# Keys, queries and values stored in DRAM in their SBUF layout, one transfer a tile

## The chip, the cores and the metric

The kernel runs on one core of a Trainium2 chip. The metric is device time in microseconds of one execution, the median over several runs. One further execution was recorded by the hardware profiler; all rows in this document come from such recordings. Arranging the inputs in DRAM is done on the host before the launch and is not in the time.

## The reference

An attention layer with a bias made by a small network, followed by two feed-forward layers. Cut to what matters here:

```python
# q, k, v: (batch 2, heads 8, seq 576, head_dim 64), float32
scores = np.matmul(q, k.transpose(0, 1, 3, 2)) / sqrt(D)
x = (psi_rel / psi_i)[..., None]            # 576 x 576, from positions alone
h = np.maximum(x @ w1 + b1, 0.0)            # hidden 32
bias = h @ w2                               # 576 x 576 x 8 heads
attn = softmax(scores + bias.transpose(2, 0, 1)[None])
x = np.matmul(attn, v)                      # -> (1152 tokens, 512)
x = (silu(x @ w_gate) * (x @ w_val)) @ w_out      # d_ff 1536
out = softplus(x @ w_in) @ w_out2                 # d_ff 2048
```

## The kernel before

The kernel has three stages. **The bias stage** (up to about 64 us) makes the 8 x 576 x 576 bias in 36 steps. A step takes four hidden tiles `r` of 128 x 576: three made by VectorE (L260), one by ScalarE (L258), each from the table `G`; 12 such tiles exist, so the hidden tiles run at most three steps ahead. TensorE multiplies them with the second layer's weights into a PSUM tile `pb` (L268, two buffers). ScalarE then copies `pb`, scaled, into a staging tile (L280, "the keep"), and a DMA on the SyncE queue spreads the 128 staged rows over the bias tiles (L284; the first four steps, which go to the bias of the mixed chunk, take two DMAs each, L287). There are six staging tiles, the halves of `early4` to `early6`, used in turn: a keep waits until the DMA of the keep six steps earlier has landed. The steps 23, 26, 31 and 33 (counted from 0) also carry one of the attention's chunks each.

**The attention stage** (to about 196 us) works through 8 units, each a pair of heads of one batch, in 72 chunks: scores (L304 for the first two units, L331 for the others), bias and row maximum (L352), exponential (L366), normalizing (L374), transposes (L401), values (L428). **The feed-forward stage** (196 us to the end) is a chain of matmuls with weights that the SyncE queue brings in (L628). The order on each engine in the bias and attention stages is the order in which the code is written.

A unit needs three kinds of input. `load` (L161 to L165) brings keys or queries of both heads into a tile of 128 partitions x 2 heads x 576: partitions 0 to 63 and 64 to 127 get the same 64 rows, by two DMAs of 64 partitions (`load_k` into `kr` or, from the third unit on, into a part of the first bias tile, so rows named `bias<-in_kT_dram` are key loads; `load_q` into `qr` or `early7`, which shows as `early<-in_qT_dram`). `load_v` (L181 to L184) brings 512 rows of the values into `v` and the last 64 into `vt`. All go through the one SyncE queue, in the order of the code: the table `G`, then keys, queries and values of the first unit, keys and queries of the second, then the 40 bias DMAs of the 36 steps, then the loads of the later units, each a chunk or more ahead of its use. The completion counters of the DMAs are used in turn, eight of them, so a DMA is issued only when the one eight issues earlier has landed (`DMAHW0` to `DMAHW7` in the rows of the order below).

Of the kernel before, what the change touches and what calls it, by code (L numbers as in the profile page):

```python
# [19 lines left out]
P = 128  # L20
B, H, S, D, HID = 2, 8, 576, 64, 32
NP = H // 2
# [27 lines left out]
ROWS = np.r_[:256, 512:S, 256:512]  # L50
# [47 lines left out]


@with_exitstack  # L100
def tile_kernel(ctx: ExitStack, tc, qT, kT, vS, wb, wg, wv, wo, wi, wo2, table, out):
    nc = tc.nc
    sp = nc.sync
    const = ctx.enter_context(tc.tile_pool(name="const", bufs=1))
# [24 lines left out]
    with ExitStack() as actx:  # L129
# [29 lines left out]
        psS = pool("psS", 2, space=PSUM)  # L159

        def load(r, src, pr, b):  # L161
            for d in range(2):
                sp.dma_start(
                    out=r[D * d : D * (d + 1)], in_=src[b, 2 * pr : 2 * pr + 2].rearrange("h d s -> d h s")
                )  # L165

        def load_k(i):
            pr, b = UNITS[i]
            kr = kp.tile([P, 2, S], F32, tag="kst", name="kr") if i < PLAIN else bias[0][:, :2]
            load(kr, kT, pr, b)  # L170
            return dict(i=i, pr=pr, b=b, kr=kr)

        def load_q(u):
            u["qr"] = early[3] if u["i"] == 1 else qraw.tile([P, 2, S], F32, tag="qr", name="qr")
            load(u["qr"], qT, u["pr"], u["b"])

        def load_v(u):
            pr, b = u["pr"], u["b"]
            v = u["v"] = vp.tile([P, 4, 3 * D], F32, name="v")
            vt = u["vt"] = vts[u["i"] % 3]  # L180
            sp.dma_start(out=v, in_=vS[b, pr, :512].rearrange("(c p) e -> p c e", p=P))  # L181
            thirds = lambda ap: ap.rearrange("p (t e) -> p t e", t=3)
            sp.dma_start(out=thirds(vt[:D])[:, ::2], in_=thirds(vS[b, pr, 512:])[:, ::2])
            sp.dma_start(out=vt[D:, D : 2 * D], in_=vS[b, pr, 512:, D : 2 * D])  # L184

        def high(h, src, by="a"):
            if by == "a":
# [298 lines left out]
        units, late = [load_k(0)], []  # L486
        load_q(units[0])
        load_v(units[0])
        units.append(load_k(1))
        load_q(units[1])  # L490
# [7 lines left out]
        def run_slot():  # L498
            nonlocal turned, done, prep, before, slot
            if slot < len(chunks):  # L500
                i, sub, n = chunks[slot]
                if n == 0:
                    for _ in prep:
                        pass
                    if (i, sub) == (1, 0):
                        load_v(units[1])
                    elif (i, sub) == (0, 1):
                        units.append(load_k(2))
                    elif sub and i + 1 < 2 * NP:
                        load_q(units[i + 1])  # L510
                        if i > 1:
                            load_v(units[i + 1])
                        prep = itertools.chain(prepare_k(units[i + 1]), prepare_q(units[i + 1], 0))
                    elif i > 1 and not sub:
                        if i + 1 < 2 * NP:
                            units.append(load_k(i + 1))
                        if i == 2:
                            load_v(units[2])
                            units[2][0].update(v=units[2]["v"], vt=units[2]["vt"])
                        prep = prepare_q(units[i], 1)  # L520
                    if i < PLAIN:
                        job(units[i], sub)
                    if i == NP and sub == 0:
                        flat = lambda ap: ap.rearrange("p a s -> p (a s)")
                        pairs[2:] = [flat(bias[c][:, 2 * a : 2 * a + 2]) for a in range(2) for c in (2, 3)]
                        mixes[1] = flat(bias[4][:, :2])[:, : 5 * P]
                        nc.gpsimd.memset(mixes[1][:, S:], 0.0)
                u = units[i][sub]
                got = scores(u, n)
# [106 lines left out]
    def as_float(n):  # L636


        x = cvp.tile([P, 2 * NK, P], F32, tag="x", name="x")
        load(2 * n + 3)  # L640
        for j in range(2):
            raw, y = loaded[2 * n + j], x[:, NK * j : NK * (j + 1)]
            hw, lw, yi = raw[:, :, :, 1], raw[:, :, :, 0], y.bitcast(I32)
            if n < NL2:
                nc.scalar.activation(y, hw.bitcast(F32), AF.Prelu, scale=2.0**-112, alpha=-(2.0**32))
            else:
                nc.scalar.activation(y, hw.bitcast(F32), AF.Copy, scale=2.0**-112)  # L647
            nc.vector.tensor_scalar(yi, yi, 3, None, op0=ALU.logical_shift_left)  # L648
            if n >= NL2:
                nc.vector.scalar_tensor_tensor(yi, hw, -(2**31), yi, op0=ALU.bitwise_and, op1=ALU.bitwise_or)  # L650
            nc.vector.scalar_tensor_tensor(yi, lw, 29, yi, op0=ALU.logical_shift_right, op1=ALU.bitwise_or)  # L651
            load(2 * n + j + 4)
        return x
# [340 lines left out]
    for k in range(2):  # L994
        t4 = row()
        h, l = [ap.bitcast(F32) for ap in X["T2"][k]]
# [50 lines left out]
    with tc.manual_schedule(engines={E.PE}):  # L1047
        quads = {"z": z}
        for q in range(4):
# [5 lines left out]
            for word in f"{OTHER if q else FIRST} {TAIL}".split():  # L1055
                who, what = word
                if who in "tu":
# [7 lines left out]
                    for i, t in enumerate(TOKENS[n]):  # L1065
                        if who == "t":
                            continue
                        a, ps = acc[t // 2][:, t % 2], held[n][:, i]
# [12 lines left out]
                getattr(quads[who], "p" + what)()  # L1081


_INS = ["qT", "kT", "vS", "wb", "wg", "wv", "wo", "wi", "wo2", "table"]


# [32 lines left out]
```

## Time and profile before

| | us |
|---|---|
| median of 3 runs | 596.39 (596.32 to 596.82) |
| the profiled execution | 596.96 |
| its span, first to last instruction | 595.0 |
| bias stage: last keep starts at | 63.07 |
| attention stage: about | 64 to 196 |
| feed-forward stage: about | 196 to 592 |

The profiled execution is 0.57 us above the median, and 1.96 us of it lie outside the span. Over the whole span TensorE is recorded as busy 97% of the time, VectorE 76%, ScalarE 63%, GpSimd 17%. These are averages over three stages with different limits, so the slices of the span and the tables by stretch say more than the averages.

### The profile page before, as it was taken

Reading aid. Unit: us, or ns where it says so; the run is one execution under the profiler, and the core shown is the slowest. Engines: PE = TensorE matmul, PEld = TensorE weight load, DVE = VectorE, ACT = ScalarE, POOL = GpSimd, SP = SyncE. Lnnn points to the kernel's source line nnn. Section 1 sums busy time; section 2 is a strip of 40 time slices with the busy share of each in tenths; the row PEclk is TensorE's granted clock in tenths of the full one; section 3 lists DMA queues with packets and bytes.
Section 4 is the critical chain, followed back from the end, with each engine's and each line's share of the span. In section 5 each row is a group of like instructions: output and inputs, shape, how many; then the busy total and the mean of one; then the engine's idle time right before and its main releaser. Section 6 shows DMA issues by size and latency. Waiting matters only on the chain.

```text
span 595.0 us, 11346 instructions
## 1 busy us (share of the span) xinstructions
PE 578.5 (97%) x4274; PEld 506.3 (85%) x4274; DVE 454.2 (76%) x972; ACT 375.5 (63%) x711; POOL 98.8 (17%) x147
## 2 busy tenths in 40 slices
PE   8789999999999999999999999999999999999997
PEld 5233569888887999999999999999989989988986
DVE  6799687788888999897789735679998976983432
ACT  6699877778988876665558424349735734733520
POOL 0000477778993000000000000000000000000000
PEclk9899999999999999999999999999999999999999
DMA  9999924334442333324226222222444240310012
GB/s 216 223 204 210 192 80 108 97 88 111 110 128 82 121 96 110 101 79 135 72 89 194 72 72 72 74 83 64 135 138 136 81 142 8 136 35 1 2 54 105
DMA packets 47414, 63.30 MB, mean 106 GB/s; under 512 B 4480, under 2 KB 35200, under 8 KB 47360
## 3 DMA queue, kind: packets, MB, share of 16 engines
q1 hardware_dynamic: 47216, 62.57, 38.2%
q8 instruction: 33, 0.54, 0.4%
q14 instruction: 21, 0.17, 0.1%
q10 hardware_dynamic: 144, 0.02, 0.0%
HBM read 49.60 MB, written 2.36 MB: 87 GB/s over the span
## 4 chain that ended last, share of the span: by engine, by line
PE 83%; DMA 6%; DVE 5%; ACT 3%; issue 1%; POOL 1%; SPq 0%; ACTq 0%; DVEq 0%; POOLq 0%
PE pw L726 37%; PE pw L1034 17%; PE pw L677 13%; PE po L428 6%; PE ps L331 4%; DMA bias<-early 4%; PE pt L401 3%; DMA early<-in_qT_dram 1%; PE pb L268 1%; PE ps L304 1%; DMA qr<-in_qT_dram 1%; ACT early L280 1%; DVE e L352 1%; ACT e L366 1%; DVE bias L352 0%
## 5 line engine op out<-in xcount | busy, mean ns | idle before, releaser
L1034 PE MATMUL pw<-oh,g2h 128*128 128x512 f32 x144 | 56.2, 390 | 0.0
L1034 PE MATMUL pw<-oh,g2l 128*128 128x512 f32 x144 | 56.2, 390 | 0.0
L1034 PE MATMUL pw<-ol,g2h 128*128 128x512 f32 x144 | 56.1, 390 | 0.0
L268 PE MATMUL pb<-r,wb_sb 128*32 128x288 f32 x576 | 46.6, 426 | 7.8 <-ACT early L280 6.8
L260 DVE TENSOR_SCALAR r<-G 128x576 f32<-128x576 f32 x108 | 47.7, 516 | 4.3 <-PE pb L268 4.0
L268 PEld LDWEIGHTS pb<-r,wb_sb 128*32 128x32 f32 x576 | 18.8, 112 | 34.6 <-ACT early L280 18.9
L677 PE MATMUL pw<-gl,sh 128*128 128x384 f32 x144 | 48.2, 335 | 0.0
L677 PE MATMUL pw<-gh,sl 128*128 128x384 f32 x144 | 48.2, 334 | 0.0
L677 PE MATMUL pw<-gh,sh 128*128 128x384 f32 x144 | 48.2, 334 | 0.0
L651 DVE SCALAR_TENSOR_TENSOR x<-raw,x 128x512 int32<-128x512 int32 x68 | 46.3, 688 | 0.9
L374 POOL TENSOR_SCALAR e<-e,sm 128x576 f32<-128x576 f32 x44 | 34.4, 793 | 73.2 <-DVE sm L371 66.9
L352 DVE CUSTOM_DVE_ANT_0 e<-ps,bias 128x576 f32<-128x576 f32 x44 | 33.0, 750 | 13.2 <-PE ps L331 7.6
L408 ACT COPY at<-pt 128x512 f32<-128x512 f32 (+2 forms) x69 | 36.4, 547 | 6.4 <-PE pt L401 5.9
L331 PE MATMUL ps<-kst,ql 128*128 128x288 f32 x120 | 37.0, 337 | 2.0 <-DVE sm L352 1.4
L428 PE MATMUL po<-at,v 128*64 128x256 f32 (+3 forms) x384 | 36.8, 332 | 1.0 <-DVE at L408 0.8
L1072 DVE TENSOR_TENSOR acc<-pw,acc 128x512 f32<-128x512 f32 x27 | 17.5, 686 | 25.1 <-PE pw L1034 25.1
L366 ACT ACTIVATE e<-e,sm 128x576 f32<-128x576 f32 x44 | 34.3, 780 | 2.7 <-DVE sm L352 1.7
L648 DVE TENSOR_SCALAR x<-x 128x512 int32<-128x512 int32 x68 | 28.8, 428 | 9.3 <-ACT x L647 5.1
L428 PEld LDWEIGHTS po<-at,v 128*64 128x64 f32 x384 | 26.7, 137 | 8.2 <-issue 1.3
L331 PE MATMUL ps<-kst,qh 128*128 128x288 f32 x120 | 32.1, 295 | 0.0
L1034 PEld LDWEIGHTS pw<-oh,g2l 128*128 128x128 f32 x144 | 27.0, 188 | 5.8
L401 PE MATMUL pt<-ident,e 128*128 128x128 f32 x188 | 31.6, 276 | 0.1
(269 smaller groups left out, 1657.4 us busy)
## 6 DMA issues: line engine op xcount, KB each, us to landing
raw<-in_wo_dram SPq DMA_DIRECT2D x28, 512.0 KB, 3.5
bias<-early SPq DMA_DIRECT2D x32, 288.0 KB, 7.5
raw<-in_wi_dram SPq DMA_DIRECT2D x16, 512.0 KB, 3.8
raw<-in_wv_dram SPq DMA_DIRECT2D x12, 512.0 KB, 4.5
raw<-in_wg_dram SPq DMA_DIRECT2D x12, 512.0 KB, 3.5
qr<-in_qT_dram SPq DMA_DIRECT2D x14, 288.0 KB, 4.1
bias<-in_kT_dram SPq DMA_DIRECT2D x12, 288.0 KB, 4.6
v<-in_vS_dram SPq DMA_DIRECT2D x8, 384.0 KB, 3.6
```

What stands on the lines that cost most here:

```text
L260: nc.vector.tensor_scalar(r, G[:, w0 : w0 + S], PB[:, n : n + 1], 0.0, op0=ALU.add, op1=ALU.max)
L268: nc.tensor.matmul(pb[32 * ct : 32 * ct + 32, hf, :HALF], W2, rs[ct][:, HALF * hf : HALF * (hf + 1)], start=True, stop=True,)
L331: nc.tensor.matmul(ps[:, hf, :HALF], u[t][:, o : o + P], kst[:, a, HALF * hf : HALF * (hf + 1)], start=i == 0, stop=i == len(parts) - 1,)
L352: nc.vector.tensor_tensor_reduce(out=e[:, :S].rearrange("p (a n) -> p a n", a=2), in0=ps[:, :, :HALF], in1=bt.rearrange("p (a n) -> p a n" ...
L366: nc.scalar.activation(e, e, AF.Exp, bias=sm[:, 0, n : n + 1], scale=-1.0, accum_out=sm[:, 1, n : n + 1])
L401: nc.tensor.transpose(pt[:, P * w : P * (w + 1)], e, ident)
L408: marks[eng, u["i"], u["sub"]] = copy(at[:, :w], pt[:, :w]).ins
L428: nc.tensor.matmul(u["po"][D * a : D * (a + 1), o : o + n], v[:, D * t : D * (t + 1)], at[:, i : i + n], start=piece == 0 and o == 0, stop ...
L651: nc.vector.scalar_tensor_tensor(yi, lw, 29, yi, op0=ALU.logical_shift_right, op1=ALU.bitwise_or)
L677: nc.tensor.matmul(ps[:, :n], w[:, k], x, start=first and k == 0 and i == 0, stop=last and k == NK - 1 and i == 2)
L726: nc.tensor.matmul(ps[:, hf, :HALF], a[:, o + k], b[:, HALF * hf : HALF * (hf + 1)], start=start and k == 0 and i == 0, stop=k == 1 and i ...
L1034: nc.tensor.matmul(ps, g, w.rearrange("p k f -> p (k f)"), start=f == 0 and i == 0, stop=f == 3 and i == 2)
```

## The change

The host stores keys and queries for each batch and head pair as 128 rows of 1152 numbers (64 rows, written twice), values as 128 rows of 768 numbers, and the last 64 value rows as a tensor of their own, `vT`. A load of keys or queries becomes one DMA of 128 partitions with one run of 4608 bytes a partition, where there were two DMAs of 64 partitions with two runs of 2304 bytes each. The DMA into `v` keeps its 128 partitions, and its runs go from four of 768 bytes to one of 3072. The two DMAs into `vt` keep their shape. Keys and queries take twice the room in DRAM; as many bytes as before are read.

```diff
         def load(r, src, pr, b):
-            for d in range(2):
-                sp.dma_start(
-                    out=r[D * d : D * (d + 1)], in_=src[b, 2 * pr : 2 * pr + 2].rearrange("h d s -> d h s")
-                )
+            sp.dma_start(out=r, in_=src[b, pr].rearrange("p (h s) -> p h s", h=2))
...
-            sp.dma_start(out=v, in_=vS[b, pr, :512].rearrange("(c p) e -> p c e", p=P))
+            sp.dma_start(out=v, in_=vS[b, pr].rearrange("p (c e) -> p c e", c=4))
             thirds = lambda ap: ap.rearrange("p (t e) -> p t e", t=3)
-            sp.dma_start(out=thirds(vt[:D])[:, ::2], in_=thirds(vS[b, pr, 512:])[:, ::2])
-            sp.dma_start(out=vt[D:, D : 2 * D], in_=vS[b, pr, 512:, D : 2 * D])
+            sp.dma_start(out=thirds(vt[:D])[:, ::2], in_=thirds(vT[b, pr])[:, ::2])
+            sp.dma_start(out=vt[D:, D : 2 * D], in_=vT[b, pr, :, D : 2 * D])
...
+    vs = np.concatenate([v[:, ::2], np.roll(v[:, 1::2], -D, 2), v[:, 1::2]], 3)
+
+    def twice(a):
+
+        a = a.reshape(B, NP, 2, S, D).transpose(0, 1, 4, 2, 3).reshape(B, NP, D, 2 * S)
+        return np.concatenate([a, a], 2)
+
...
-        "qT": np.stack([q[:, h][:, ROWS if h % 2 else slice(None)] for h in range(H)], 1).transpose(0, 1, 3, 2),
-        "kT": k.transpose(0, 1, 3, 2),
-        "vS": np.concatenate([v[:, ::2], np.roll(v[:, 1::2], -D, 2), v[:, 1::2]], 3),
+        "qT": twice(np.stack([q[:, h][:, ROWS if h % 2 else slice(None)] for h in range(H)], 1)),
+        "kT": twice(k),
+        "vS": vs[:, :, :512].reshape(B, NP, 4, P, 3 * D).transpose(0, 1, 3, 2, 4).reshape(B, NP, P, 12 * D),
+        "vT": vs[:, :, 512:],
```

On TensorE, VectorE, ScalarE and GpSimd the same instructions stand in the same order; only the DMA counters that they wait on differ. The SyncE queue has 14 rows fewer. Its start before the change, from the first key load to the second bias DMA of the first step (`kr` keys, `qr` and `early` queries, `bias<-early` the bias of the steps; the rows with x2 are the two halves):

```order
L163 DMA kr<-in_kT_dram 64x2x576 x2
L163 DMA qr<-in_qT_dram 64x2x576 x2
L181 DMA v<-in_vS_dram 128x4x192
L183 DMA vt_96<-in_vS_dram 64x2x64 [waits DMAHW0_49,Pool_49]
L184 DMA vt_96<-in_vS_dram 64x64 [waits DMAHW1_49]
L163 DMA kr<-in_kT_dram 64x2x576 [waits DMAHW2_49]
L163 DMA kr<-in_kT_dram 64x2x576 [waits DMAHW3_49]
L163 DMA early_116<-in_qT_dram 64x2x576 [waits DMAHW4_49]
L163 DMA early_116<-in_qT_dram 64x2x576 [waits DMAHW5_49]
L287 DMA bias_89<-early_113 16x4x576 [waits DMAHW6_49,Activation_49]
L287 DMA bias_89<-early_113 16x4x576 [waits DMAHW7_49]
```

And the same place after it:

```order
L162 DMA kr<-in_kT_dram 128x1152
L162 DMA qr<-in_qT_dram 128x1152
L178 DMA v<-in_vS_dram 128x768
L180 DMA vt_96<-in_vT_dram 64x2x64 [waits Pool_49]
L181 DMA vt_96<-in_vT_dram 64x64
L162 DMA kr<-in_kT_dram 128x1152 [waits DMAHW0_49]
L162 DMA early_116<-in_qT_dram 128x1152 [waits DMAHW1_49]
L284 DMA bias_89<-early_113 16x4x576 [waits DMAHW2_49,Activation_49]
L284 DMA bias_89<-early_113 16x4x576 [waits DMAHW3_49]
```

Four issues went away, and each load stands behind an older DMA in the turn of the counters: the second unit's queries (`early`) waited for a landing of the first unit's queries and now wait for the first part of the table `G`.

## Rows read from the trace of the kernel before

**Rows 1.** The page, chain that ended last: shares of the span by engine.
```profile
PE 83%; DMA 6%; DVE 5%; ACT 3%; issue 1%; POOL 1%; SPq 0%; ACTq 0%; DVEq 0%; POOLq 0%
```
**Rows 2.** The page: 40 slices of 14.9 us, TensorE clock and DMA share in tenths.
```profile
PEclk9899999999999999999999999999999999999999
DMA  9999924334442333324226222222444240310012
```
**Rows 3.** Windows: each engine's busy us (instructions), granted clock, DMA share, GB/s.
```profile
3.00:5.00 2.00, 2.00 (x11) 2.00 (x11) 0.23 (x2) 0.00 (x0) 0.00 (x0) 1.00 0.99 364
5.00:17.00 12.00, 11.96 (x133) 6.17 (x134) 11.96 (x29) 10.10 (x15) 0.00 (x0) 1.00 1.06 230
...
17.00:20.00 3.00, 0.85 (x12) 0.19 (x4) 3.00 (x9) 0.00 (x0) 0.00 (x0) 1.00 1.04 248
...
28.00:40.00 12.00, 10.22 (x147) 3.75 (x144) 11.98 (x29) 11.65 (x19) 0.00 (x0) 1.00 1.04 206
...
72.00:196.00 124.00, 120.99 (x1059) 99.68 (x1056) 100.53 (x301) 101.54 (x243) 90.94 (x128) 1.00 0.36 99
196.00:592.00 396.00, 395.37 (x2545) 377.34 (x2543) 294.43 (x525) 213.99 (x372) 0.00 (x0) 1.00 0.28 90
```
**Rows 4.** Timeline of ScalarE, keeps 4, 6, 7, 24 and 36: start, us, idle before.
```profile
12.79 0.73 ACT L280 ACTIVATE early<-pb,G 128x576 f32<-128x576 f32 x1
...
15.37 0.74 ACT L280 ACTIVATE early<-pb,G 128x576 f32<-128x576 f32 x1
...
21.26 0.74 ACT L280 ACTIVATE early<-pb,G 128x576 f32<-128x576 f32 x1 [4.49 <-DMA bias<-early]
...
45.64 0.74 ACT L280 ACTIVATE early<-pb,G 128x576 f32<-128x576 f32 x1
...
63.07 0.74 ACT L280 ACTIVATE early<-pb,G 128x576 f32<-128x576 f32 x1 [0.32 <-PE pb L268]
```
**Rows 5.** Chain that ended last, pieces in order of time, first 20 us.
```profile
3.04 7.48 DMA qr<-in_qT_dram
...
10.54 8.62 DMA early<-in_qT_dram
```
**Rows 6.** The page, DMA issues: count, KB each, median us to landing.
```profile
qr<-in_qT_dram SPq DMA_DIRECT2D x14, 288.0 KB, 4.1
...
v<-in_vS_dram SPq DMA_DIRECT2D x8, 384.0 KB, 3.6
...
kr<-in_kT_dram SPq DMA_DIRECT2D x4, 288.0 KB, 7.4
...
early<-in_qT_dram SPq DMA_DIRECT2D x2, 288.0 KB, 8.5
```
**Rows 7.** Timeline of the SyncE queue: start and us of issues, first 20 us.
```profile
9.27 1.86 SPq L163 DMA_DIRECT2D early<-in_qT_dram  x2
12.11 7.59 SPq L287 DMA_DIRECT2D bias<-early  x8
```
**Rows 8.** Timeline of VectorE in the bias stage: start, us, idle before.
```profile
8.83 11.67 DVE L260 TENSOR_SCALAR r<-G 128x576 f32<-128x576 f32 x27
24.03 1.38 DVE L260 TENSOR_SCALAR r<-G 128x576 f32<-128x576 f32 x3 [3.53 <-PE pb L268]
25.91 18.67 DVE L260 TENSOR_SCALAR r<-G 128x576 f32<-128x576 f32 x42 [0.50 <-PE pb L268]
```
**Rows 9.** Waits of compute engines for DMAs, 64 to 196 us: us, times, longest.
```profile
DVE e L352 <- DMA bias<-early: 0.3, 1, 0.3
...
PEld po L428 <- DMA vt<-in_vS_dram: 0.2, 1, 0.2
...
PEld po L428 <- DMA bias<-in_kT_dram: 0.2, 1, 0.2
```
**Rows 10.** Timeline of the SyncE queue: the third unit's queries, two halves.
```profile
75.82 1.79 SPq L163 DMA_DIRECT2D qr<-in_qT_dram  x2
```
**Rows 11.** Tile `qr` from 70 to 175 us: its halves' time from issue to landing.
```profile
DMA to landing us min/median/max: 3.5/4.0/5.0
```
**Rows 12.** Timeline of VectorE: first use of the third unit's queries.
```profile
82.53 0.29 DVE L190 CAST qh<-qr 128x256 fp32r<-128x256 f32 x1
```

More of the change, by code (lines that the diff above doesn't have):

```diff
@@ L100, in tile_kernel @@
 @with_exitstack
-def tile_kernel(ctx: ExitStack, tc, qT, kT, vS, wb, wg, wv, wo, wi, wo2, table, out):
+def tile_kernel(ctx: ExitStack, tc, qT, kT, vS, vT, wb, wg, wv, wo, wi, wo2, table, out):
     nc = tc.nc
@@ L1081, in tile_kernel @@
                 getattr(quads[who], "p" + what)()
-_INS = ["qT", "kT", "vS", "wb", "wg", "wv", "wo", "wi", "wo2", "table"]
+_INS = ["qT", "kT", "vS", "vT", "wb", "wg", "wv", "wo", "wi", "wo2", "table"]
 def kernel(q, k, v, w1, b1, w2, moe_w_gate, moe_w_val, moe_w_out, moe2_w_in, moe2_w_out):
```

## Prediction

> **What bounds the kernel now.** I began with the chain that ended last by engine [rows 1]: TensorE holds 83% of it, but DMA holds 6%, which is some 36 us of the span. [...] From 3 to 5 us, when the table `G` comes in over 128 partitions, 364 GB/s flow at a DMA share of 0.99. From 5 to 17 us, when keys, queries and values of the first two units come in, the share is as full (1.06) but only 230 GB/s flow. From 28 to 40 us, with the steps' bias DMAs alone, it is 206 GB/s at 1.04. The DMA engines are the limit in all three; what differs is what they get done.
>
> What it costs the compute engines stands in ScalarE's timeline [rows 4]. Keeps 4 and 6 start at 12.79 and 15.37 us, so two steps take 2.58 us, 1.29 a step: the pace of the compute engines. Keep 7 is the first that needs a staging tile back, and it starts at 21.26 us, after 4.49 us of idling for a bias DMA. That DMA stood in the queue behind the loads. Between 17 and 20 us TensorE is busy for 0.85 us of 3 [rows 3], and VectorE, which may run only three steps ahead, stands 3.53 us soon after [rows 8]. From keep 7 to keep 24 the start moves from 21.26 to 45.64 us, 17 steps at 1.434 us. A step's 288 KB (295 thousand bytes) at 206 GB/s take 1.43 us, so this stretch goes at the pace of the DMAs. From keep 24 to keep 36 (63.07 us) four attention chunks ride along.
>
> After that DMA matters to nobody: from 72 to 196 us its share is 0.36 [rows 3], and the compute engines' waits for DMAs from 64 us on are three, 0.7 us in sum [rows 9]. From 196 us to the end TensorE is busy 395.37 of 396 us [rows 3]. A microsecond taken off the end of the bias stage should therefore arrive at the end of the kernel.
>
> **The change, part by part.** First the transfers of the first 20 us. Four halves of `kr`, two of `qr`, two of `early` and one `v` are 8 x 288 + 384 = 2688 KB [rows 6], 2.75 million bytes. At 230 GB/s they take 12.0 us, which is the stretch from 5 to 17 us. The nearest row for a load of 128 partitions with runs of over 3000 bytes is that of `G`, 364 GB/s, and with it they take 7.6 us: **4.4 us less**. The trace doesn't show a key load over 128 partitions, so I bound it. At the low end is a middle between the two rates, 297 GB/s: 9.3 us, 2.7 us less. At the high end, `G`'s stretch also carries the small rows of the weights, so a pure rate may be higher; at 400 GB/s the loads would take 6.9 us, 5.1 us less. I keep 4.4, as `G` has the form that the loads get.
>
> [...]
>
> What does the bias stage make of it? Keep 7 waits for the first step's landing, which comes 4.4 us earlier, at 21.26 - 4.4 = 16.9 us. By the compute pace it could start at 15.37 + 1.29 = 16.66 us. So of the 4.49 us of idling about 0.2 is left. From there the bias DMAs, 1.43 us each, are slower than the compute engines, 1.29; the whole row of DMAs lies 4.4 us earlier, and the keeps follow it as before. Keep 24 comes at 41.2 us in place of 45.64. The steps with attention chunks then take their 17.4 us as before, and keep 36 starts at about 58.6 us. VectorE could follow: it idles 3.53 + 0.50 us in three rows alone [rows 8], and it does 27 hidden tiles in 11.67 us, 1.30 us a step, below 1.43. If the loads go faster than `G` did, VectorE and ScalarE, which have little more than 5 us to give, cap the gain at about 5.5 us.
>
> The clock dip of the second slice [rows 2] follows TensorE's idling from 17 to 20 us. If that goes, the dip should go; while it lasts TensorE isn't what the keeps wait for longest, so I price this at nothing to 0.5 us of gain (an estimate, from a dip that takes a fifth off one slice and a stage that TensorE does not bound).
>
> Second, the issues. Half the key and query issues go, some 0.6 us of the SyncE queue each (two of `early` take 1.86 us with a wait between) [rows 7]. Today the second query load waits for the first's landing (7.48 us, and the `early` load's own 8.62 us follow in the chain) [rows 5]; afterwards it waits for `G`, so the queue fills sooner. That by itself gives nothing, since the DMA engines are full all that time. The first bias DMA is issued at 12.11 us [rows 7]; with the loads done at about 5 + 7.6 = 12.6 us it finds its way free. The first four steps' eight bias issues now wait for landings of the loads, which are all there by about 14 us, before the queue of DMAs could run dry. No compute engine waits on an issue.
>
> Third, the later units. Each load there gets shorter too, and nobody waits for it [rows 9]: 0, with 0.7 us as the bound. `vT` as its own tensor and the doubled room in DRAM: the bytes read are the same, 0.
>
> The sum is 4.4 us in the bias stage, plus about 0.1 for the clock and the small waits: **4.5 us**. The profiled execution would be 596.96 - 4.5 = 592.5 us; against the median of 596.39 us that is 591.9 us.
>
> **The rivals.** *Partly given back.* Compute engines and DMAs pace within 10% of each other (1.29 and 1.43 us), and the loads may not reach `G`'s rate beside other work. At 297 GB/s the gain is 2.7 us; with another microsecond lost where the three engines wait on each other in the chunk-carrying steps, 1.7. Time: 593.7 to 594.7 us. For it: four steps at the end carry extra work, and no slack shows there. Against: those steps take what they take now, whenever they begin.
>
> *It is not the 128 partitions.* `G` may be fast for another reason, such as being first in an empty queue, and the loads stay at 230 GB/s. Then only issues go, which nobody waits for: 596.3 us, within 0.2%. Against it speaks that the DMA share is full in both stretches, so an empty queue explains nothing. [...]
>
> *Slower: a whole tile lands too late in the attention stage.* A first half lands 3.5 to 5.0 us after its issue [rows 11], and the consumer needs both. The third unit's queries are issued at 75.82 us [rows 10] and used at 82.53 us [rows 12], 6.7 us later. If one transfer of 576 KB took over 6.7 us, VectorE's cast would wait, in each of the six later units. At the 8.5 us that a load takes in the full first stretch [rows 6], that is 1.8 us x 6 = 10.8 us lost against 4.5 won: 602.7 us. Against it: the DMA share is 0.36 there, and two halves, issued 0.6 us apart, make it today.
>
> **How the numbers follow.** The forecast, gain 3.5 to 5.5 us with 4.5 the likeliest: 0.74. Partly given back: 0.12. No effect: 0.09. Slower: 0.05. The range reaches from the cap of 5.5 us plus 0.3 us for the spread of the runs (590.6 us) to the middle of the second case (594.2 us), which holds about 0.8. About 0.2% (1.2 us) is what a measurement of this kernel can tell from no change. The first case and nearly all of the second are faster by more than that, 0.86; the third is within it, 0.09; the fourth is slower, 0.05.
>
> **What would show it.** The stretch from 5 to 12 us should show 350 GB/s or more in place of 230. ScalarE's wait of 4.49 us before keep 7 should fall under 0.5 us, with keep 7 near 16.9 us, keep 24 near 41 us and keep 36 near 58.6 us. TensorE's dip in the clock should be gone. From keep 36 to the end as many microseconds as before should pass. If the rate is reached and keep 36 does not move, the step from loads to keeps was wrong; if keep 36 moves by 4.5 us and the end does not, the rigid shift of the later stages was.

## The result and the profile after

The changed kernel takes **590.92 us** (median of 4 runs, 589.93 to 591.70) beside 596.36 us for the kernel before (595.30 to 596.82): a ratio of 0.9911, 95% interval 0.9891 to 0.9930, so 5.4 us less, with 4.2 to 6.5 us inside the interval. A second set of runs gave 590.64 us, ratio 0.9908 (0.9892 to 0.9924). Forecast were 591.9 us, with a range from 590.6 to 594.2.

The profiled execution has a span of 589.9 us, 5.1 less than before. Its slices of 14.7 us, the TensorE clock and the DMA share, answer to [rows 2]:

```profile
PEclk9999999999999999999999999999999999999999
DMA  8999624332242433242244221322344240300012
```

The dip in the clock is gone, and the fifth slice, in which the DMA engines were still full before (the row of before begins with five nines), is at 6 tenths. The table by stretch (the busy time of TensorE, weight loads, VectorE, ScalarE and GpSimd, then granted clock, DMA share, GB/s) answers to [rows 3]:

```profile
5.00:12.00 7.00, 6.96 (x76) 3.68 (x77) 6.96 (x17) 5.82 (x9) 0.00 (x0) 1.00 1.02 392
14.00:20.00 6.00, 5.94 (x76) 2.74 (x67) 6.00 (x15) 5.46 (x9) 0.00 (x0) 1.00 0.87 215
20.00:28.00 8.00, 6.66 (x95) 2.51 (x96) 8.00 (x20) 7.51 (x13) 0.00 (x0) 1.00 1.04 201
28.00:40.00 12.00, 9.96 (x138) 3.53 (x132) 11.63 (x27) 11.63 (x17) 0.00 (x0) 1.00 1.05 206
40.00:52.00 12.00, 10.91 (x134) 4.47 (x134) 10.68 (x26) 11.64 (x20) 0.84 (x1) 1.00 1.05 210
```

From 5 to 12 us 392 GB/s flow, at the same full share at which 230 flowed before. Seven microseconds at that rate are 2.74 million bytes, nearly the whole of the first two units' loads (2.75 million), which took 12 us; their last packets land later, at 14.55 us in this profile. The bias DMAs alone are unchanged, 206 GB/s.

ScalarE's timeline shows keeps 1, 7, 9, 10, 24 and 36 (start, duration, idle time before), for [rows 4]:

```profile
7.73 0.74 ACT L277 ACTIVATE early<-pb,G 128x576 f32<-128x576 f32 x1 [0.56 <-PE pb L265]
...
16.17 0.74 ACT L277 ACTIVATE early<-pb,G 128x576 f32<-128x576 f32 x1
...
19.41 0.74 ACT L277 ACTIVATE early<-pb,G 128x576 f32<-128x576 f32 x1 [0.54 <-DMA bias<-early]
21.19 0.74 ACT L277 ACTIVATE early<-pb,G 128x576 f32<-128x576 f32 x1 [0.38 <-DMA bias<-early]
...
40.71 0.73 ACT L277 ACTIVATE early<-pb,G 128x576 f32<-128x576 f32 x1
...
58.38 0.74 ACT L277 ACTIVATE early<-pb,G 128x576 f32<-128x576 f32 x1 [0.32 <-PE pb L265]
```

Keep 7 doesn't wait any more; 0.54 and 0.38 us of waiting are left two and three keeps later. VectorE's hidden tiles run through without the stands of 3.53 and 0.50 us of [rows 8] (72 tiles in one row, 0.437 us each):

```profile
8.33 31.47 DVE L257 TENSOR_SCALAR r<-G 128x576 f32<-128x576 f32 x72
```

Keep 36 starts 4.69 us earlier (63.07 to 58.38). Of this 0.50 us lies before keep 1 (8.23 to 7.73), since the small table of weights `wb_sb`, for which VectorE waits at the start (until 4.77 us before, 4.27 us here), landed half a microsecond sooner in this execution. In the profiles of the experiments keep 1 starts anywhere from 8.07 to 9.01 us, whatever the form of the loads, so these 0.5 us are a spread of executions. The number to compare is therefore the time from keep 1 to keep 36: 54.84 us before, 50.65 us after, 4.2 us less. After that the attention stage gives 0.6 us more, and the rest of the kernel takes 0.3 us longer: the last VectorE addition starts at 586.36 us, and at 591.43 before.

### The profile page after: what moved, and what is told of

Its sections match the earlier page's. It is cut to its first block, busy times and chain, and to the rows that moved or that the text cites. A ratio compares the mean times of both kernels' runs of the same rounds, so it can differ in the third digit from the quotient of the medians.

```text
span 589.9 us, 11310 instructions
## 1 busy us (share of the span) xinstructions
PE 577.0 (98%) x4274; PEld 506.0 (86%) x4274; DVE 453.5 (77%) x972; ACT 375.3 (64%) x711; POOL 98.6 (17%) x147
## 4 chain that ended last, share of the span: by engine, by line
PE 80%; DVE 7%; DMA 5%; ACT 4%; POOL 1%; issue 1%; SPq 1%; ACTq 0%; POOLq 0%; DVEq 0%
PE pw L723 37%; PE pw L1031 17%; PE pw L674 11%; PE po L425 6%; PE ps L328 4%; DMA bias<-early 4%; PE pt L398 3%; DMA early<-in_qT_dram 2%; PE pb L265 2%; PE ps L301 1%; ACT early L277 1%; DVE e L349 1%; DVE bias L349 1%; ACT e L363 1%; ACT at L405 1%
## 5 line engine op out<-in xcount | busy, mean ns | idle before, releaser
L265 PE MATMUL pb<-r,wb_sb 128*32 128x288 f32 x576 | 45.3, 412 | 4.6 <-ACT early L277 4.0
L425 PE MATMUL po<-at,v 128*64 128x256 f32 (+3 forms) x384 | 36.8, 332 | 1.0 <-DVE at L405 0.8
```

The lines of the kernel that those rows point to most:

```text
L265: nc.tensor.matmul(pb[32 * ct : 32 * ct + 32, hf, :HALF], W2, rs[ct][:, HALF * hf : HALF * (hf + 1)], start=True, stop=True,)
L425: nc.tensor.matmul(u["po"][D * a : D * (a + 1), o : o + n], v[:, D * t : D * (t + 1)], at[:, i : i + n], start=piece == 0 and o == 0, stop ...
```

## Experiments

Each was timed beside the kernel before. "Keep 1 to 36" is the time from the start of keep 1 to that of keep 36 in its profile. A row of a timeline gives an idle time only where it is over 0.15 us, so a keep without one may still have waited a little.

**One DMA, 128 partitions, the old run length.** Edit to the kernel before, with the key and query rows written twice in DRAM:

```diff
-            for d in range(2):
-                sp.dma_start(
-                    out=r[D * d : D * (d + 1)], in_=src[b, 2 * pr : 2 * pr + 2].rearrange("h d s -> d h s")
-                )
+            sp.dma_start(out=r, in_=src[b, 2 * pr : 2 * pr + 2].rearrange("h p s -> p h s"))
```

> Keys and queries by one DMA of 128 partitions each, but with two runs of 2304 bytes a partition as before; values as before. Theory, partitions: the loads' rate follows from the span of 128 partitions, so from 5 to 12 us some 390 GB/s flow, keep 36 starts at 58 to 59 us, and the time is 591 us. Rival, run length: without runs of 4608 bytes the rate stays at 230 GB/s, keep 36 at 63 us, 596.4 us. Rival, DMA count (fewer issues and counters, so the queue fills sooner): as with the first theory, 591 us.

**Two DMAs of 64 partitions, the new run length.** Edit to the kernel before, with both heads' rows side by side in DRAM:

```diff
             for d in range(2):
                 sp.dma_start(
-                    out=r[D * d : D * (d + 1)], in_=src[b, 2 * pr : 2 * pr + 2].rearrange("h d s -> d h s")
+                    out=r[D * d : D * (d + 1)], in_=src[b, pr].rearrange("d (h s) -> d h s", h=2)
                 )
```

> Keys and queries by two DMAs of 64 partitions as before, but with one run of 4608 bytes a partition; values as before. Theory, partitions: 230 GB/s from 5 to 17 us, keep 36 at 63 us, 596.4 us. Rival, run length: 390 GB/s, keep 36 at 58 to 59 us, 591 us. Rival, DMA count: 596.4 us.

**Two DMAs of 128 partitions, one head each.** Edit to the kernel before, DRAM as in the first experiment:

```diff
-            for d in range(2):
-                sp.dma_start(
-                    out=r[D * d : D * (d + 1)], in_=src[b, 2 * pr : 2 * pr + 2].rearrange("h d s -> d h s")
-                )
+            for h in range(2):
+                sp.dma_start(out=r[:, h], in_=src[b, 2 * pr + h])
```

> Keys and queries by two DMAs of 128 partitions, one head each, runs of 2304 bytes: as many issues, counters, runs and bytes as before, only the partitions of one DMA differ. Theory, partitions: some 390 GB/s from 5 to 12 us, keep 36 at 58 to 59.5 us, 591 to 592 us. Rival, run length: 596.4 us. Rival, DMA count: 596.4 us.

These three stand together. Times: 591.25 us (ratio 0.9921, 0.9906 to 0.9935), 596.26 us (1.0001, 0.9989 to 1.0013), 591.35 us (0.9925, 0.9910 to 0.9940). The stretch from 5 to 12 us and keep 7 of the first:

```profile
5.00:12.00 7.00, 6.95 (x66) 3.59 (x69) 6.96 (x16) 5.08 (x8) 0.00 (x0) 1.00 1.06 375
...
16.90 0.74 ACT L277 ACTIVATE early<-pb,G 128x576 f32<-128x576 f32 x1
```

Of the second, with long runs in halves:

```profile
5.00:12.00 7.00, 6.96 (x67) 3.95 (x70) 6.96 (x16) 5.13 (x8) 0.00 (x0) 1.00 1.08 254
...
20.80 0.74 ACT L280 ACTIVATE early<-pb,G 128x576 f32<-128x576 f32 x1 [3.83 <-DMA bias<-early]
```

Of the third, split by head:

```profile
5.00:12.00 7.00, 6.96 (x66) 3.89 (x69) 6.89 (x16) 5.02 (x8) 0.00 (x0) 1.00 1.06 370
...
16.97 0.74 ACT L278 ACTIVATE early<-pb,G 128x576 f32<-128x576 f32 x1
```

From 5 to 12 us the loads in halves stayed slow with the long runs, 254 GB/s, and the loads over 128 partitions were fast with the short ones, 375 GB/s, also as two DMAs and with all the old turns of the counters, 370 GB/s. In these runs the partitions that one DMA spans decide, and the DMA count has no part that these runs could tell. Run length has at most a small one: over 128 partitions the short runs flowed at 370 and 375 GB/s from 5 to 12 us, and in the profiles with the long runs of keys, queries and values together it was 392 to 406 GB/s. That is about half a microsecond of the loads' seven; the times (591.25 and 591.35 us here, 590.64 and 590.92 us for the change) differ by as much, within their intervals. The title's words "one transfer a tile" name what was done and not what helped.

One thing goes with the partitions in every run: by halves the same rows of DRAM are read twice, and over 128 partitions every row stands in DRAM twice and each copy is read once. No run separates the two. The trace of the kernel before speaks against this rival:

```profile
5.00:6.00 1.00, 1.00 (x10) 1.00 (x8) 0.96 (x4) 0.44 (x1) 0.00 (x0) 1.00 0.99 249
6.00:10.00 4.00, 3.96 (x37) 1.65 (x37) 4.00 (x10) 3.44 (x6) 0.00 (x0) 1.00 1.04 234
```

From 5 to 6 us 249 thousand bytes come in, less than the first half alone has (288 KB, 295 thousand bytes). If the queue serves the halves in their order, the rate has fallen before any row is read a second time. The bias DMAs, which read nothing from DRAM, are as slow, 206 GB/s.

**The values alone.** Edit to the changed kernel, with the key and query tensors of before:

```diff
-            sp.dma_start(out=r, in_=src[b, pr].rearrange("p (h s) -> p h s", h=2))
+            for d in range(2):
+                sp.dma_start(
+                    out=r[D * d : D * (d + 1)], in_=src[b, 2 * pr : 2 * pr + 2].rearrange("h d s -> d h s")
+                )
```

> Only the values in the new layout, one run of 3072 bytes a partition; keys and queries as before. Theory, partitions: the values had 128 partitions already, so 0 to 0.4 us off keep 36 (63.07 us) and 596.0 to 596.4 us. Rival, run length: the values are 0.39 of 2.75 million bytes, so about a seventh of the 5.4 us, 0.8 us: 595.6 us.

595.66 us, ratio 0.9991 (0.9981 to 1.0001). Keep 7 still waits 3.59 us:

```profile
20.32 0.74 ACT L280 ACTIVATE early<-pb,G 128x576 f32<-128x576 f32 x1 [3.59 <-DMA bias<-early]
```

The median lies where the rival had it, and below the theory's 596.0 to 596.4 us; keep 36 starts at 61.84 us, 1.2 and 0.6 us before those of the two profiles of the kernel before. But the interval runs from 1.1 us less to no difference, so an effect of the runs of 3072 bytes is likely and not settled; 0.6 us is what the medians give. 0.3 to 0.6 us also lie between the first experiment (591.25) and the change (590.92 and 590.64). The rates point the same way: from 5 to 12 us 392 and 406 GB/s flow in the two profiles of the change, and 375 and 370 in those of the first and third experiments, where values, keys and queries have their short runs.

**The first two units alone, and the later six alone.** Edit to the changed kernel; the reverse has `pr > 0`:

```diff
-            sp.dma_start(out=r, in_=src[b, pr].rearrange("p (h s) -> p h s", h=2))
+            if pr == 0:
+                sp.dma_start(out=r, in_=src[b, pr].rearrange("p (h s) -> p h s", h=2))
+                return
+            for d in range(2):
+                sp.dma_start(
+                    out=r[D * d : D * (d + 1)], in_=src[b, pr, :D].rearrange("d (h s) -> d h s", h=2)
+                )
```

> Keys and queries in the new form for the first two units only; those of the six later units by two DMAs of 64 partitions (from the same packed rows); values as after the change. Theory: the gain is made in the first 20 us and carried to the end, so keep 36 starts at 58 to 58.6 us and the time is 590.9 to 591.4 us. Rival, the later units take part: in the two profiles the attention stage took 0.6 us off between chunk 40 and chunk 60, so about 0.6 us is missing here, 591.5 us or more.

> The reverse: the first two units' keys and queries by two DMAs of 64 partitions, the six later units' in the new form; values as after the change. Theory: only what the values alone gave is left, 595.7 to 596.3 us, keep 36 at 61.5 to 63.1 us. Rival, the later units take part: 0.6 us more, 595.1 us.

590.96 us (0.9915, 0.9900 to 0.9929) and 595.70 us (0.9992, 0.9977 to 1.0008). Keeps 7 and 36 with the first units new:

```profile
17.45 0.74 ACT L283 ACTIVATE early<-pb,G 128x576 f32<-128x576 f32 x1
...
57.46 0.74 ACT L283 ACTIVATE early<-pb,G 128x576 f32<-128x576 f32 x1 [0.31 <-PE pb L271]
```

And with the later ones new:

```profile
20.30 0.74 ACT L283 ACTIVATE early<-pb,G 128x576 f32<-128x576 f32 x1 [3.43 <-DMA bias<-early]
...
61.37 0.74 ACT L283 ACTIVATE early<-pb,G 128x576 f32<-128x576 f32 x1 [0.32 <-PE pb L271]
```

The gain is made by two units of eight, in the first 20 us; in both, keep 36 comes a little before the range that was expected for it, and the times lie inside theirs. The first kernel's keep 1 to 36 took 48.45 us (9.01 to 57.46), 2.2 us less than in the change's own first profile. A second profile of both kernels shows how much of that is spread.

**Both kernels again, unchanged.**

> The changed kernel as it is, once more, for a second profile beside more times. In its first profile keep 1 to keep 36 took 50.65 us, the keeps waited 0.9 us for bias DMAs, and the last packets of the loads ended later than most. Theory, that profile is one of a spread, since the compute engines' pace (48.45 us) and the DMAs' lie close: 48.5 to 50.7 us here, 590.5 to 591.3 us. Rival, the one long transfer with its later landing holds the counters and costs 2 us each time: 50.65 us within 0.2.

> The kernel before, once more, for a second profile. In its first one keep 1 to keep 36 took 54.84 us; in the two kernels that load keys and queries of the first units by halves it took 53.2 and 53.0 us. Theory, the first profile was at the slow end of its spread (596.96 us beside a median of 596.3): 53.0 to 54.0 us here and 596.2 us. Rival, the runs of 768 and 2304 bytes cost that 1.7 us: 54.8 us within 0.2.

590.64 us (ratio above) and 596.12 us (1.0002, 0.9992 to 1.0012). The loads' stretch and the one behind it, and keeps 1, 24 and 36 of the changed kernel, second profile; no wait of a keep for a DMA is over 0.15 us in it:

```profile
5.00:12.00 7.00, 6.96 (x72) 4.25 (x72) 6.96 (x16) 5.48 (x9) 0.00 (x0) 1.00 1.03 406
14.00:20.00 6.00, 6.00 (x80) 3.15 (x80) 6.00 (x15) 6.00 (x11) 0.00 (x0) 1.00 1.02 221
...
8.35 0.74 ACT L277 ACTIVATE early<-pb,G 128x576 f32<-128x576 f32 x1 [0.84 <-PE pb L265]
...
39.54 0.74 ACT L277 ACTIVATE early<-pb,G 128x576 f32<-128x576 f32 x1
56.93 0.74 ACT L277 ACTIVATE early<-pb,G 128x576 f32<-128x576 f32 x1 [0.33 <-PE pb L265]
```

Waits that short are there all the same. Keeps 16 to 24 of this profile start 1.41 us apart in the mean (28.29 to 39.54 us), near the 1.43 us of a bias DMA, and the chain that ended last goes from one keep through a bias DMA to keep 24 (start, us):

```profile
30.95 0.75 ACT early L277
...
31.71 7.74 DMA bias<-early
...
39.54 0.74 ACT early L277
```

Keeps 1, 7 and 36 of the kernel before, second profile:

```profile
8.29 0.74 ACT L280 ACTIVATE early<-pb,G 128x576 f32<-128x576 f32 x1 [0.56 <-PE pb L268]
20.90 0.74 ACT L280 ACTIVATE early<-pb,G 128x576 f32<-128x576 f32 x1 [4.06 <-DMA bias<-early]
...
62.40 0.74 ACT L280 ACTIVATE early<-pb,G 128x576 f32<-128x576 f32 x1 [0.33 <-PE pb L268]
```

Keep 1 to 36 is 48.58 us after and 54.11 us before: 5.5 us in this pair, 4.2 in the first. The 2 us by which the two profiles of the changed kernel differ are thus a spread between executions, as the theory had it: in the first one the DMAs of the bias ran late, for which the part on the counters gives a reason, and the steps went at their pace nearly all the way. For the kernel before the second profile lies between theory and rival, 0.1 us above the one and 0.5 us below the other.

**The first unit's values at step 31.** Edit to the changed kernel:

```diff
         load_q(units[0])
-        load_v(units[0])
...
                 if i in EARLY:
+                    if i == EARLY[2]:
+                        load_v(units[0])
+                        units[0][0].update(v=units[0]["v"], vt=units[0]["vt"])
                     run_slot()
```

> After the change, and the first unit's values (432 KB in three DMAs) are not loaded ahead of the bias DMAs but with step 31. Theory, the row of bias DMAs begins when the loads are through and sets the keeps from there: it begins 0.44 million bytes / 392 GB/s = 1.1 us earlier, keep 24 comes at 39.6 us in place of 40.71, keep 36 at 57.3 us, the time is 589.9 us. Rival, after the change the compute engines set the pace: keep 24 and keep 36 stay within 0.3 us, 590.9 us.

590.76 us (0.9911, 0.9896 to 0.9925), the same as the change, where the theory had 589.9 us. Its keep 1 to 36 took 48.45 us (8.53 to 56.98), and no wait of a keep for a DMA is listed. Against the change's second profile (48.58 us, keep 36 at 56.93) taking another 0.44 million bytes away from the front gained nothing, so the rival is right in the time; against its first one (58.38) keep 36 did come earlier. With the loads at 392 GB/s or more the compute engines' pace is nearly reached.

**Another order of the steps.** Edit to the changed kernel, and to the kernel before:

```diff
-        order = [32, 33, 34, 35, *range(32)]
+        order = [32, 33, 34, 35, *(8 * c + t for c in range(4) for t in (0, 4, 1, 5, 2, 6, 3, 7))]
```

> After the change, and within each bias tile the eight steps come in the order 0, 4, 1, 5, 2, 6, 3, 7, so that neighbouring bias DMAs write partitions that lie 4 or 3 apart in place of 1. Theory: every bias DMA reaches the same 16 partitions at a time as before and the engines take them one after the other, so 206 GB/s and 591 us stay. [...]

> The kernel before, by halves and with its old layout, but with the alternating order of steps. Theory, the loads' 12 us and the row of bias DMAs are two costs one behind the other: keep 7 still waits until 20 to 21.3 us, then the steps go at the compute engines' 1.29 us in place of 1.43 and keep 36 comes 1.5 to 2.5 us earlier, 593.9 to 594.8 us; the change is then still worth 3.5 to 4.5 us on top (e8 against this one). Rival, faster bias DMAs drain the queue while the loads come in and take most of what the change gave: below 592.5 us.

On the changed kernel 590.20 us (0.9901, 0.9886 to 0.9916), on the kernel before 594.93 us (0.9981, 0.9969 to 0.9993). Two stretches of the changed kernel with this order, and its last keep:

```profile
28.00:40.00 12.00, 12.00 (x153) 5.42 (x152) 12.00 (x29) 11.92 (x19) 0.00 (x0) 1.00 1.00 230
40.00:52.00 12.00, 11.70 (x136) 4.95 (x132) 11.96 (x31) 11.27 (x18) 1.19 (x1) 1.00 0.75 203
...
56.52 0.74 ACT L277 ACTIVATE early<-pb,G 128x576 f32<-128x576 f32 x1 [0.32 <-PE pb L265]
```

The same stretches of the kernel before with this order, and its keep 7:

```profile
28.00:40.00 12.00, 10.95 (x152) 3.99 (x156) 12.00 (x29) 12.00 (x19) 0.00 (x0) 1.00 0.97 247
40.00:52.00 12.00, 11.09 (x148) 4.62 (x139) 11.70 (x30) 12.00 (x21) 1.20 (x1) 1.00 0.81 222
...
21.40 0.74 ACT L280 ACTIVATE early<-pb,G 128x576 f32<-128x576 f32 x1 [4.51 <-DMA bias<-early]
```

Here the first expectation's theory fell, by which 206 GB/s were to stay: with the order alone the bias DMAs went at up to 247 GB/s, and from 40 to 52 us 203 GB/s needed only 0.75 of the DMA engines' time, where 210 needed 1.05. In the kernel before this gains 1.1 us (0.4 to 1.8), somewhat less than expected, and keep 7 waits as long as ever: the loads' delay and the pace of the bias DMAs are two costs in a row. On top of this order the change still gives 4.7 us (594.93 to 590.20), a little more than the 3.5 to 4.5 us expected. On the changed kernel the order takes keep 1 to 36 to 48.45 us; its time and the change's own can't be told apart.

**Both edits on the changed kernel.**

> After the change, with the first unit's values at step 31 and the alternating order of steps together. Theory, in both apart the keeps already go at the compute engines' pace (48.45 us from keep 1 to keep 36 in either): nothing is left to add, 48.4 us again and 590.2 us. Rival, the two gains add, since each takes its own part off the DMAs: 0.2 us less than the alternating order alone, 590.0 us or below.

590.30 us (0.9904, 0.9887 to 0.9920), keep 1 to 36 again 48.45 us (8.11 to 56.57). Nothing adds up any more. Four profiles (the first units alone, the values later, the other order, and both edits) end at the same 48.45 us and list no wait of a keep for a DMA: that is the compute engines' own time. Which of them sets it was not tested; in the row from 28 to 40 us above TensorE and VectorE are busy for 12.00 of 12 us and ScalarE for 11.92.

## Why the prediction was right

**What bounds.** Right: the DMA engines in the first 20 us, by their rate and not by their share. Of the rivals, DMA count gave nothing, and run length about half a microsecond by the medians, not settled. One reading was too wide: the three waits for DMAs, 0.7 us in sum, are those from 64 to 196 us and not all "from 64 us on". In the feed-forward stage ScalarE waits three times for weights, 8.8 us in sum before and 8.2 after, while TensorE stays busy there [rows 3], so the forecast didn't suffer by it.

**The loads' rate.** That loads over 128 partitions would go at about `G`'s rate was right, the term a little small. `G`'s 364 GB/s were taken, for 7.6 us; 392 and 406 GB/s came in the two profiles, so 7.0 us or less. The term of 4.4 us should have been 5.0. The one row of `G` was a sample of a spread: from 3 to 5 us it is 364 GB/s in the first profile of before and 398 in that of the change. The experiment by head shows the difference with two DMAs a load in either form, 370 GB/s over 128 partitions against 254 by halves. By halves 221 to 254 GB/s flowed from 5 to 12 us in six profiles; the values, which span 128 partitions, and the end of `G` lie in that stretch, and from 6 to 10 us, mostly halves, it was 234 in the first profile of before. Why the halves go slower was not shown.

**From the loads to keep 7.** Right: 16.2 us (16.9 foretold, 0.5 of it the earlier start), with no wait. Keep 7 came at the compute engines' pace, as the 16.66 us of the forecast had it.

**From keep 7 to keep 24.** This step was mis-sized. The forecast had it at the DMAs' 1.434 us a step, 24.4 us. In the first profile it took 24.54 us, in the second 23.03 us (16.51 to 39.54), and 21.9 to 22.1 us in the four profiles at 48.45 us. Six staging tiles let the compute engines run ahead on a queue that no longer starts late. Here lie up to 2 us, which the forecast gave only to its range. In the second pair of profiles 4.4 us are gained up to keep 7 and 1.1 us from there to keep 24 (24.09 to 23.03), 5.5 in all; in the first pair the first part alone carries the gain. That the medians show 5.4 us and not 4.5 is most likely this part; the other runs have no profile to tell.

**The cap.** Put at 5.5 us; the floor of 48.45 us says 5.7 to 6.4 us against the two profiles of before. The lower end of the range, 590.6 us, came from this cap, and the two medians of 590.92 and 590.64 us lie just inside it. That the range held is in this part luck.

**The counters.** The forecast said that the queue would not run dry behind the loads' landings. In the first profile it did: the second unit's queries land at 14.55 us, the SyncE queue waits for them, and the DMA share is 0.87 from 14 to 20 us. The chain shows the place (start, us) and where it leads, to keep 10:

```profile
5.37 9.18 DMA early<-in_qT_dram
...
14.57 6.52 DMA bias<-early
...
21.19 0.74 ACT early L277
```

Three steps of 1.29 us after keep 7 (16.17 us) would have put keep 10 at 20.04 us, so it came about 1.1 us late, which the forecast had at nothing. It doesn't come in every execution: in the second profile the share is 1.02 there, and in the kernel with only the first units new, where keep 1 started 1.28 us later, a share of 0.81 held no keep up.

**The clock.** Right. In the first profile of before the granted clock is at 0.50 of full speed from 23 to 25 us, after TensorE's idling; from 20 to 28 us its mean is 0.57 to 0.79 in the profiles with halves in the first units, and 1.00 in every profile with the first units' loads over 128 partitions. What the dip by itself cost, priced at nothing to 0.5 us, no run tells apart. The stretch in the second profile of before:

```profile
20.00:28.00 8.00, 6.31 (x60) 2.73 (x64) 3.80 (x10) 5.84 (x9) 0.00 (x0) 0.57 1.03 206
```

**The rigid shift.** Right, within 0.6 us. Chunk 40 to chunk 60 of the attention took 37.4 us in some profiles and 36.8 in others: 37.4 in all seven profiles with halves in the first or the later units, 36.8 in six of the seven with every load of keys and queries over 128 partitions, and 37.4 in the seventh, with both edits of the last experiment. So the form of the loads alone doesn't set it; what does was not found. The rival of a gain partly given back (593.7 to 594.7 us) didn't come, nor the slower one, whole tiles landing too late: in the two profiles of the change a weight-load wait of 0.2 us is the longest for a key load after 60 us.

## What to carry to other kernels

When DMA engines are full, compare GB/s between stretches of the same share before counting DMAs: 230 beside 364 GB/s told that the form of the transfer was at fault. Try one DMA over all 128 partitions first, and a split, if there has to be one, along the free dimension: from 5 to 12 us the loads over 128 partitions came here at 370 to 406 GB/s, the 370 with a split by head, and those in halves of 64 partitions at 221 to 254. A shorter transfer paid here only where a queue was waited for, for two units of eight, and only until the next pace, the compute engines' 1.29 us a step, was reached.

## What was not expected of the hardware

The order of the bias DMAs changed their rate. From the fifth step on each bias DMA writes 16 partitions that lie 8 apart. With neighbours shifted by one partition they ran at 206 GB/s and a full share (1.05 from 28 to 40 us in the change); with neighbours shifted by four and three in turn, at 203 GB/s and a share of 0.75 from 40 to 52 us, and in the kernel before at up to 247 GB/s. Two kernels show it, the change and the one before. Why this order is faster was not shown, as the rows give the DMA engines only in the mean.
